# An S4 layer and a gated MLP on one core: one long convolution through DRAM replaced by two causal blocks of 1024 tokens with dense DFTs on chip, and a decay table in polar form

## The chip, the cores and the metric

The kernel runs on one core of one Trainium2 chip. The metric is the device time of one execution in microseconds (us); a figure for a kernel is the median of its runs. The span in a profile is the time from the first to the last instruction.

The engines are PE (matrix products), DVE (elementwise work), ACT (table functions and copies), POOL and SP (issues most DMAs). "PEld" is the load of PE's weights, which overlaps PE.

## The reference

One sequence of L = 2048 tokens, D = 640 channels, N = 128 states per channel, MLP width F = 1728, bf16 in and out:

```python
def _A_ref(u, ...):                       # S4 layer
    dt = exp(log_dt)[:, None]
    P = exp((dt * A)[:, :, None] * l)     # A complex, D x N; l = 0..2047
    K = einsum("dn,dnl,dn->dl", Cc, P, dt * Bc).real     # one kernel of 2048 taps per channel
    y = irfft(rfft(pad(u)) * rfft(pad(K)))[:L]           # causal convolution along the tokens
    return y + u * Dskip

h  = x + _A_ref(layernorm(x))
h2 = h + (sigmoid(n @ w_gate) * (n @ w_up)) @ w_down     # n = layernorm(h)
```

## The kernel before

The channels are handled in four chunks of 160. Per chunk, the taps come from two tables of powers, A (32 exponents) and B (21 exponents), multiplied on PE. Table A is built on DVE by doubling: from 5 seeds, each step multiplies the powers known so far by one of them.

```python
def chain_a(c):                                   # table A by doubling, all on DVE
    for d0, n, s0, b in A_STEPS:                  # n = 1, 3, 7, 15
        ...
        for ri in range(2):
            V(t[:, ri], A[:, ri, :, s0:s1, :], bc(A[:, 1, :, b:b + 1, :], [P, G, n, 4]), ALU.mult)
        for ri in range(2):
            V(A[:, ri, :, d0:d1, :], A[:, ri, :, s0:s1, :], bc(A[:, 0, :, b:b + 1, :], [P, G, n, 4]), ALU.mult)
        V(A[:, 0, :, d0:d1, :], A[:, 0, :, d0:d1, :], t[:, 1], ALU.subtract)
        V(A[:, 1, :, d0:d1, :], A[:, 1, :, d0:d1, :], t[:, 0], ALU.add)
```

The convolution is one transform of length 4096, in two stages, and its data go through DRAM between the stages, forward and back:

```python
def u_s1():                                       # forward, stage 1
    for r in range(16):
        ...                                       # matmuls with F1, copies on ACT
        sy.dma_start(d1u[:, r]..., stg[:])        # to DRAM
def u_s2(half):                                   # forward, stage 2
    for gr in range(8):
        sy.dma_start(a2g[:], dv[...])             # back from DRAM
        sy.dma_start(W2[...], cd["W2"][...])      # twiddles, loaded each time
        ...                                       # matmuls of 64 columns of weights
        nc.scalar.copy(xu[:, QPOS[q], :, :], ps[:, :, 0:UH])
def kspec(c, kv, xu, mks, dve_add):
    def front(i0, nq, tag):                       # kernel spectrum and products
        sy.dma_start(W3[...], cd["W3"][...])
        ...                                       # 5 x 2 matmuls of 160 columns per group
        nc.scalar.copy(xk, ps)
        nc.vector.tensor_tensor(t1[:], xq, xk[:], ALU.mult)
        nc.vector.tensor_tensor(t2[:], xq, xk[:, :, ::-1, :], ALU.mult)
    def back(qp, prods, W3, extra):               # inverse, stage 1
        ...
        sy.dma_start(d2[c][4 * qp:4 * qp + 4]..., stg[:])     # to DRAM
```

The second inverse stage (`is2_row`) and the skip `u * Dskip` (rows on DVE) stand in the MLP, token group by token group. The MLP has four turns of 512 tokens: gate and up matmuls, sigmoid on ACT, their product `ml_hm` on DVE, the down matmuls.

Of the kernel before, what the change touches and what calls it, by code (L numbers as in the profile page):

```python
# [9 lines left out]
F32, BF16, I32 = DT.float32, DT.bfloat16, DT.int32  # L10
# [5 lines left out]
D = 640  # L16
MAGIC = 12582912.0
SIN_SCALE = float(np.nextafter(np.float32(2.0 * PI), np.float32(0.0))) * 2.0 ** -32
CH = ((0, 160), (160, 160), (320, 160), (480, 160))
NC = len(CH)  # L20
WM = max(w for _, w in CH)
UH = 320
LAG = 2


B_VAL = [0, 4, 2, 6, 1, 5, 3, 7, 256, 260, 258, 262, 512, 516, 768, 772, 1024, 1280, 1536, 1792, 2048]
A_EXP = [16, 8, 4, 2, 1, 3, 6, 5, 7] + [8 + x for x in (4, 2, 1, 3, 6, 5, 7)] + [16 + x for x in (8, 4, 2, 1, 3, 6, 5, 7)] + [24 + x for x in (4, 2, 1, 3, 6, 5, 7)] + [0]
A_SHIFT = (7, 6, 5, 4, 3)
M_SHIFT = (0, 1, 2, 8, 9, 10)

A_STEPS = ((5, 1, 4, 3), (6, 3, 3, 2), (9, 7, 2, 1), (16, 15, 1, 0))
B_STEPS = ((1, 2, (0, 1, 1), 2), (2, 4, (0, 2, 1), 1), (4, 8, (0, 4, 1), 0), (8, 12, (0, 4, 1), 3), (12, 16, None, 4),
           (16, 18, (0, 16, 8), 5), (18, 21, (12, 17, 2), 5))
QORD = [16] + list(range(16))
QPOS = {q: i for i, q in enumerate(QORD)}


def host_consts():
    tau = 2 * np.pi
    k32 = np.arange(32)  # L40

    F1 = np.zeros((2, 32, 4, 4, 32))
    ang = tau * np.outer(k32, k32) / 64
    re, im = np.cos(ang), -np.sin(ang)
    im[:, 0] = np.cos(tau * k32 * 32 / 64)
    for q in range(4):
        F1[0, :, q, q, :] = re
        F1[1, :, q, q, :] = im
    F1 = F1.reshape(2, 128, 128).transpose(1, 0, 2)

    l2a = (16 * np.arange(4)[None, :] + np.arange(16)[:, None]).reshape(-1)
    k1 = np.arange(34)[:, None]
    k2 = np.arange(64)[None, :]
    phi = tau * l2a[:, None, None] * (k1 + 64 * k2)[None] / 4096
    c, sn = np.cos(phi), np.sin(phi)
    W2 = np.zeros((2, 64, 2, 34, 64))
    W2[0, :, 0], W2[1, :, 0], W2[0, :, 1], W2[1, :, 1] = c, sn, -sn, c
    W2[1, :, :, 0] = 0
    W2[1, :, 0, 32], W2[1, :, 1, 32] = c[:, 32], -sn[:, 32]
    W2[0, :, :, 32] = 0  # L60
    W2[:, :, :, 33] = 0

    kp, kk2 = np.arange(128) >> 6, np.arange(128) & 63
    q17 = np.arange(17)[None, :, None]
    l2b = np.arange(64)[None, None, :]
    psi = tau * l2b * (2 * q17 + kp[:, None, None] + 64 * kk2[:, None, None]) / 4096
    c, sn = np.cos(psi), np.sin(psi)
    W3a = np.concatenate([c, sn], axis=2)
    W3b = np.concatenate([-sn, c], axis=2)
    W3a[0:64, 0, 64:], W3b[0:64, 0, 64:] = 0, 0  # L70
    W3a[0:64, 16], W3b[0:64, 16] = np.concatenate([0 * c[0:64, 16], c[0:64, 16]], 1), np.concatenate([0 * c[0:64, 16], -sn[0:64, 16]], 1)
    W3 = np.stack([W3a, -W3a, W3b], axis=1)

    ang = tau * np.outer(k32, k32) / 64
    wre = 2 * np.cos(ang)
    wre[0] = 1
    wim = -2 * np.sin(ang)
    wim[0] = np.cos(tau * 32 * k32 / 64)
    W4 = np.zeros((32, 2, 2, 2, 32, 4))
    for qi in range(2):  # L80
        for qp in range(2):
            W4[:, 0, qi, qp, :, 2 * qi + qp] = wre / 4096
            W4[:, 1, qi, qp, :, 2 * qi + qp] = wim / 4096
    W4 = W4.reshape(128, 2, 128)
    sel = np.zeros((128, 4, 128))
    for i in range(4):
        sel[0:i + 1, i, 127] = 1.0
    lr = np.arange(2048).astype(np.float32).astype(ml_dtypes.bfloat16).astype(np.int64)
    f = np.arange(34)[:, None] + 64 * np.arange(64)[None, :]
    E = np.exp(-2j * np.pi * (np.arange(2048)[:, None] * f.reshape(1, -1) % 4096) / 4096)  # L90
    S = np.zeros((2049, f.size), np.complex128)
    np.add.at(S, lr, E)
    S = S.reshape(2049, 34, 64)
    S[:, 33] = 0
    M = np.zeros((17, 4, 32, 2, 5, 128))
    a = np.arange(32)
    for m in range(4):
        for j in range(5):
            blk = S[B_VAL[4 * j + m] + 8 * np.array(A_EXP)].reshape(32, 17, 128).transpose(1, 0, 2)
            M[:, m, :, 0, j] = blk.real  # L100
            M[:, m, :, 1, j] = blk.imag

    pick = np.zeros((128, 4, 32))
    for c in range(4):
        pick[4 * a + c, c, a] = 1.0
    last = np.zeros((128, 4, 4))
    for c in range(4):
        last[124 + c, c, :] = 1.0
    return {"pick": pick.reshape(128, -1), "last": last.reshape(128, -1), "ident": np.eye(128), "F1": F1.reshape(128, -1), "W2": W2.reshape(128, 2, 17, 2, 64)[:, :, QORD].transpose(0, 2, 1, 3, 4).reshape(128, -1), "W3": W3[:, :, QORD].transpose(0, 2, 1, 3).reshape(128, -1),
            "W4": W4.reshape(128, -1), "sel": sel.reshape(128, -1), "M": M.reshape(17, 128, 1280)[QORD].transpose(1, 0, 2).reshape(128, -1)}  # L110
# [27 lines left out]
def full_kernel(tc, ins, out):  # L138
    nc = tc.nc
    sc = Scope(tc)  # L140
    sy = nc.sync
    x2d = ins["A_u"].rearrange("b l d -> (b l) d")
    o2d = out.rearrange("b l d -> (b l) d")
    xv, ov = x2d.rearrange("(p r) d -> p r d", r=16), o2d.rearrange("(p r) d -> p r d", r=16)
# [3 lines left out]
    d1u = dram.tile([2, 16, P, D], BF16, name="d1u")  # L148
    d2 = [dram.tile([32, P, w], BF16, name=f"d2_{i}") for i, (_, w) in enumerate(CH)]

    cp = sc.pool("consts", bufs=1, side="right")
    tabp = sc.pool("tables", bufs=1, side="right")
    xp = sc.pool("xp", bufs=1)
    xup = sc.pool("xup", bufs=2)
    stp = sc.pool("stg", bufs=3)
    ktp = sc.pool("kts", bufs=2)
    kw2 = sc.pool("kw2", bufs=2)
    w3p = sc.pool("w3", bufs=3)
# [3 lines left out]
    def cload(pool, n, shape):  # L162
        t = pool.tile(shape, BF16, name="c_" + n)
        flat = t[:] if len(shape) == 2 else t[:].rearrange("p a b -> p (a b)") if len(shape) == 3 else t[:].rearrange("p a b c -> p (a b c)")
        sy.dma_start(flat, cd[n])
        return t

    u = xp.tile([P, 16, D], BF16, name="u", tag="X0")
    ef = xp.tile([P, 7, D], F32, name="ef", tag="X1")
# [3 lines left out]
    def load_u(rg):  # L173
        sy.dma_start(u[:, 4 * rg:4 * rg + 4, :], xv[:, 4 * rg:4 * rg + 4, :])
# [8 lines left out]
    for rg in range(1, 4):  # L183
        load_u(rg)
    F1 = cload(cp, "F1", [P, 2, P])
    W4 = cload(cp, "W4", [P, 2, P])
    sel = cload(cp, "sel", [P, 4, P])
    pick = cload(cp, "pick", [P, 4, 32])
    last = cload(cp, "last", [P, 4, 4])
    uh = cp.tile([4, D], BF16, name="uhead")  # L190
    kr = cp.tile([4, D], F32, name="klast_f")

    nc.scalar.activation(dl[:, 1], dl[:, 0], AF.Exp)
    diag = stp.tile([P, 5, 128], BF16, name="diag", tag="st")
    nc.vector.tensor_tensor(diag[:], bc(ident[:].rearrange("p (o n) -> p o n", o=1), [P, 5, 128]), bc(dl[:, 1].rearrange("p (c o) -> p c o", o=1), [P, 5, 128]), ALU.mult)
# [4 lines left out]
    def scaled(terms):  # L200
        pt = ps2.tile([P, 2, 512], F32, name="pt", tag="p2")
        pf = pt[:].rearrange("p a b -> p (a b)")
        for c in range(5):
            for i, (src, dg) in enumerate(terms):
                nc.tensor.matmul(pf[:, 128 * c:128 * c + 128], lhsT=src[:, c, :], rhs=dg[:, c, :], start=(i == 0), stop=(i == len(terms) - 1))  # L205
        return pf[:, 0:D]
# [4 lines left out]
    ph = scaled([(raw[:, 0, 1], diag)])  # L211
    TURN = 2.0 ** 32 / (2.0 * PI)
    nc.vector.tensor_scalar(rnd, ph, TURN, MAGIC * 2.0 ** 32, ALU.mult, ALU.add)
    nc.vector.tensor_scalar(rnd, rnd, MAGIC * 2.0 ** 32, None, ALU.subtract)
    phi = tabp.tile([P, D], I32, name="phi")
    nc.vector.scalar_tensor_tensor(phi[:], ph, TURN, rnd, ALU.mult, ALU.subtract)

    T = {}

    def exps(c):  # L220
        o, w = CH[c]
        T["E"] = E = tabp.tile([P, 11, WM], BF16, name="tabE")
        for i, k in enumerate(M_SHIFT + A_SHIFT):
            nc.scalar.activation(E[:, i, 0:w], lre[:, o:o + w], AF.Exp, scale=float(2 ** k))
# [3 lines left out]
    def cb_product():  # L228
        c1, c2 = ef[:, 3:5], ef[:, 5:7]
        B, C = raw[:, 1], raw[:, 2]  # L230
        f = lambda t: t.rearrange("p a b c -> p a (b c)")
        g = lambda t: t.rearrange("p b c -> p (b c)")
        nc.vector.tensor_tensor(c1, f(B), f(C), ALU.mult)
        nc.vector.tensor_tensor(c2[:, 0], g(B[:, 0]), g(C[:, 1]), ALU.mult)
        nc.vector.tensor_tensor(c2[:, 1], g(B[:, 1]), g(C[:, 0]), ALU.mult)
        blk = lambda t: t.rearrange("p (b c) -> p b c", c=128)
        for ri, (t, dg) in enumerate(((c1, (0, 1)), (c2, (0, 0)))):
            nc.scalar.copy(CB[:, ri, :], scaled([(blk(t[:, i]), diagf[:, dg[i]]) for i in range(2)]))

    NDV = 8  # L240
    mv = cp.tile([P, 16, 2], F32, name="mv")
    rstd = cp.tile([P, 16], F32, name="rstd")
    nmr = cp.tile([P, 16], F32, name="nmr")
# [196 lines left out]
    def kspec(c, kv, xu, mks, dve_add):  # L440
# [52 lines left out]
        for i, *pw in queue:  # L493
            back(i, *pw, None if i else extra)
            yield
# [347 lines left out]
```

## Time and profile before

| | before |
|---|---|
| time, median of 3 runs | 430.27 us (429.46 to 431.82) |
| span in the profile | 425.9 us |
| front: up to the first gate matmul | 229.1 us |
| MLP: from there to the end | 196.8 us |
| moved by DMA | 52.03 MB |

I cut the span where the first gate matmul starts (the table of stretches is cut 0.2 us later, at 229.3), since different engines limit the two sides. The table of stretches of the kernel before gives, per stretch, the busy time of each engine with its count of instructions, then the granted PE clock (as a share of full speed), the DMA share and GB/s:

```profile
core 0: us, PE busy (x) PEld busy (x) DVE busy (x) ACT busy (x) POOL busy (x), PEclk, DMA share, GB/s
0.00:229.30 229.30, 157.75 (x1926) 120.03 (x1928) 188.30 (x445) 167.00 (x309) 8.94 (x31) 0.84 0.58 169
229.30:425.90 196.60, 191.18 (x1089) 101.59 (x1100) 94.59 (x188) 47.20 (x75) 4.71 (x5) 0.99 0.23 68
```

In the MLP PE is busy 191 of 197 us at nearly full clock, which makes it the limit there. Over the whole front no engine is full: DVE has 188 of 229 us, ACT 167. DVE's other 41 us lie mostly at the two ends: from 40 to 180 us it is busy 132 of 140 us. The DMAs show in the chain of waits of the kernel before (shares of the span by engine), and in what PE's matmuls wait for, here three groups (line, engine, operation, out and in, count; busy us and mean ns; idle before it and what ended that):

```profile
PE 55%; DVE 23%; DMA 11%; ACT 5%; issue 2%; POOL 1%; SPq 1%; DVEq 0%; ACTq 0%; POOLq 0%
...
L451 PE MATMUL ps_xk<-kv,mk 128*128 128x160 bf16 x680 | 52.4, 236 | 2.2 <-ACT kv L416 1.2
...
L479 PE MATMUL ps_g<-t,W3g 64*128 64x160 bf16 x462 | 25.3, 244 | 12.1 <-DVE t L458 5.2
...
L382 PE MATMUL ps_s<-a2g,W2g 128*64 128x320 bf16 x136 | 17.4, 388 | 10.9 <-DMA W2g<-s4c_W 7.5
```

DMA has 11% of the chain, 47 us: apart from the first load of `u` (5.1 us), these are the trips through DRAM and the twiddles. The largest groups of table A, from the list of groups with each shape apart:

```profile
L331 DVE TENSOR_TENSOR tabA<-tabA 128x2400 bf16<-128x2400 bf16 x8 | 11.2, 1402 | 0.0
L329 DVE TENSOR_TENSOR tS<-tabA 128x2400 bf16<-128x2400 bf16 x8 | 10.9, 1402 | 0.0
```

Summed over its shapes, the doubling of table A is 65 us of DVE, a third of DVE's work in the front.

### The profile page before, as it was taken

How to read it: one execution, taken by the hardware profiler on the slowest of the kernel's cores; microseconds unless marked ns; L12 is line 12 of the kernel's file. 1: busy time of each engine (PE TensorE's matmuls, PEld its weight loads, DVE VectorE, ACT ScalarE, POOL GpSimd, SP SyncE). 2: the span in 40 equal slices, each digit the busy share in tenths (PEclk: the TensorE clock that was granted, in tenths of full speed). 3: DMA queues.
4: the chain of work that ended last, by engine and by line, in shares of the span. 5: the costliest groups of instructions: out<-in, count | busy, mean ns of one | idle time of the engine just before them, and what ended most of it. 6: DMA issues, size and time to landing. Idle time of an engine off the chain costs nothing.

```text
span 425.9 us, 7734 instructions
## 1 busy us (share of the span) xinstructions
PE 348.9 (82%) x3013; PEld 221.6 (52%) x3028; DVE 282.9 (66%) x633; ACT 214.2 (50%) x383; POOL 13.6 (3%) x36
## 2 busy tenths in 40 slices
PE   1615656697968979789647999999999999999996
PEld 0602235286728858678424444654466445654463
DVE  4978999979998999937723589426932386223331
ACT  6799987995798955544525525322210212012210
POOL 0011000000000000000002001000100000000000
PEclk9976658599788989989986999999999999999999
DMA  8564649865472551649628998010001000010001
GB/s 190 223 237 147 214 146 333 267 186 124 108 219 81 127 130 45 160 106 256 190 51 261 306 299 222 0 63 1 1 2 53 11 0 2 2 62 0 2 15 48
DMA packets 71108, 52.03 MB, mean 122 GB/s; under 512 B 42016, under 2 KB 68896, under 8 KB 71072
## 3 DMA queue, kind: packets, MB, share of 16 engines
q1 hardware_dynamic: 71072, 51.53, 41.3%
q8 instruction: 24, 0.39, 0.4%
q14 instruction: 12, 0.10, 0.1%
HBM read 38.41 MB, written 13.11 MB: 121 GB/s over the span
## 4 chain that ended last, share of the span: by engine, by line
PE 55%; DVE 23%; DMA 11%; ACT 5%; issue 2%; POOL 1%; SPq 1%; DVEq 0%; ACTq 0%; POOLq 0%
PE ml_po L767 13%; PE ml_pg L731 13%; PE ml_pu L731 12%; DMA W2g<-s4c_W 4%; PE ps_xk L451 3%; DVE tS L329 3%; PE pk L401 3%; DVE tabA L331 2%; DVE t L458 2%; DVE t L459 2%; PE ps_y L505 2%; PE pt L205 2%; PE ml_pt L713 2%; DVE tS L351 2%; DMA d1u<-s_stg 2%
## 5 line engine op out<-in xcount | busy, mean ns | idle before, releaser
L739 ACT ACTIVATE ml_sg<-ml_pg 128x512 bf16<-128x512 f32 x52 | 31.0, 597 | 119.6 <-PE ml_pg L731 119.6
L740 DVE TENSOR_TENSOR ml_hm<-ml_pu,ml_sg 128x512 bf16<-128x512 f32 x52 | 35.5, 682 | 49.2 <-PE ml_pu L731 49.1
L731 PE MATMUL ml_pg<-lnT,Wg 128*128 128x512 bf16 x251 | 65.2, 383 | 0.5
L731 PE MATMUL ml_pu<-lnT,Wu 128*128 128x512 bf16 x256 | 64.8, 380 | 0.4 <-issue 0.2
L767 PE MATMUL ml_po<-Wd,ml_hm 128*128 128x320 bf16 x416 | 60.1, 299 | 0.0
L451 PE MATMUL ps_xk<-kv,mk 128*128 128x160 bf16 x680 | 52.4, 236 | 2.2 <-ACT kv L416 1.2
L451 PEld LDWEIGHTS <-mk 128*128 128x128 bf16 x680 | 48.0, 99 | 5.6 <-issue 2.7
L767 PEld LDWEIGHTS <-ml_hm 128*128 128x128 bf16 x416 | 39.8, 98 | 17.5 <-issue 2.1
L731 PEld LDWEIGHTS <-Wu 128*128 128x128 bf16 x260 | 25.5, 98 | 30.4 <-issue 0.3
L731 PEld LDWEIGHTS <-Wg 128*128 128x128 bf16 x260 | 25.3, 99 | 29.1 <-issue 1.1
L780 DVE TENSOR_TENSOR ml_out<-ml_po,h 128x640 bf16<-128x640 f32 x16 | 13.2, 825 | 38.6 <-PE ml_po L767 21.1
L479 PE MATMUL ps_g<-t,W3g 64*128 64x160 bf16 x462 | 25.3, 244 | 12.1 <-DVE t L458 5.2
L362 PE MATMUL ps_s<-u,c_F 128*128 128x320 bf16 x64 | 18.0, 402 | 19.7 <-ACT s_stg L363 14.3
L453 ACT CAST xk<-ps_xk 128x640 bf16<-128x640 f32 (+1 forms) x36 | 23.7, 664 | 17.0 <-PE ps_xk L451 14.5
L479 PEld LDWEIGHTS <-W3g 64*128 64x128 bf16 x462 | 17.8, 99 | 18.1 <-issue 11.3
L482 ACT CAST g_stg<-ps_g 128x640 bf16<-128x640 f32 x32 | 22.3, 697 | 8.6 <-DMA d<-g_stg 5.2
L382 PE MATMUL ps_s<-a2g,W2g 128*64 128x320 bf16 x136 | 17.4, 388 | 10.9 <-DMA W2g<-s4c_W 7.5
L401 PE MATMUL pk<-tabB,tabA 128*128 128x84 bf16 x320 | 21.1, 235 | 4.1 <-DVE tabA L332 1.7
L362 PEld LDWEIGHTS <-c_F 128*128 128x128 bf16 x64 | 7.4, 118 | 29.3 <-issue 21.0
L401 PEld LDWEIGHTS <-tabA 128*128 128x128 bf16 x320 | 18.4, 120 | 8.2 <-issue 7.7
L384 ACT CAST xu<-ps_s 128x640 bf16<-128x640 f32 x34 | 21.3, 700 | 2.6 <-PE ps_s L382 2.5
L458 DVE TENSOR_TENSOR t<-xu,xk 128x640 bf16<-128x640 bf16 (+1 forms) x36 | 16.9, 470 | 6.8 <-ACT xk L453 6.6
(119 smaller groups left out, 493.7 us busy)
## 6 DMA issues: line engine op xcount, KB each, us to landing
W3g<-s4c_W SPq DMA_DIRECT2D x32, 192.0 KB, 2.8
d1u<-s_stg SPq DMA_DIRECT2D x16, 320.0 KB, 2.3
a2g<-d1u SPq DMA_DIRECT2D x16, 320.0 KB, 4.3
d<-g_stg SPq DMA_DIRECT2D x32, 160.0 KB, 2.5
g<-d SPq DMA_DIRECT2D x16, 320.0 KB, 6.0
mk<-s4c_M SPq DMA_DIRECT2D x5, 960.0 KB, 7.2
u<-in_A_u_dram SPq DMA_DIRECT2D x4, 640.0 KB, 5.3
h<-in_A_u_dram SPq DMA_DIRECT2D x4, 640.0 KB, 5.9
```

The lines of the kernel that those rows point to most:

```text
L362: nc.tensor.matmul(ps[:, ri, 0:UH], lhsT=F1[:, ri, :], rhs=u[:, r, o:o + UH], start=True, stop=True)
L384: nc.scalar.copy(xu[:, QPOS[q], :, :], ps[:, :, 0:UH])
L401: nc.tensor.matmul(pk[:, i, :], lhsT=A[:, ri, g].rearrange("p e c -> p (e c)"), rhs=B[:, ri, :, 4 * g:4 * g + 4], start=(ri == 0), stop=(r ...
L451: nc.tensor.matmul(ps[:, qi, ri * w:ri * w + w], lhsT=mks[i0 + qi][:, ri, j, :], rhs=kv[:, j, :], start=(j == 0), stop=(j == 4))
L453: nc.scalar.copy(xk[:].rearrange("p q r w -> p q (r w)"), ps[:, 0:nq, 0:2 * w])
L458: nc.vector.tensor_tensor(t1[:], xq, xk[:], ALU.mult)
L479: nc.tensor.matmul(ps[:, kpar, qi * w:qi * w + w], lhsT=Wt[sl, ti, wi, :], rhs=t[sl, ti, ro, :], start=(i == 0), stop=(i == cnt[kpar] - 1) ...
L482: nc.scalar.copy(stg[:].rearrange("p (q k) w -> p k q w", k=2), ps[:, :, 0:2 * w].rearrange("p k (q w) -> p k q w", q=2))
L731: nc.tensor.matmul(ps[:], lhsT=W[:, dc, f0:f0 + 128], rhs=rhs, start=(dc == 0), stop=(dc == 4))
L739: nc.scalar.activation(sg[:], pg[:], AF.Sigmoid)
L740: nc.vector.tensor_tensor(hm[:, ft, :], pu[:], sg[:], ALU.mult)
L767: nc.tensor.matmul(po[k][:, c, 0:320], lhsT=hm[:, ft, 128 * lr:128 * lr + 128], rhs=Wd[:, ft, 320 * c:320 * c + 320], start=(start and ft ...
```

## The change

Its intent: replace the trips through DRAM by dense DFTs of 1024 tokens on chip, two causal blocks of them; build table A with much less DVE work, as magnitude times cosine and sine; and move part of the convolution under the MLP, where DVE and ACT have room.

- A block's tokens and their reversal are added and subtracted (`fold`), and multiplied with a dense real matrix G (`forward`). Block 0's spectrum stays in SBUF; block 1's goes to DRAM for later use.
- Table A's entry is exp(8k Re) times cos and sin of a phase; exponents 16 to 31 reuse the same cosines and sines (`table_a`). For that the phases are counted from the middle of the table, and the phase of the middle is put into the product C times B.
- `Dskip` is added to tap 0 by one small matmul.
- Only the first block's products and inverse (`kspec`, `inv0`) stand before the MLP. Those of the second block (`products1`, `inverse1`) are given a priority 1200 places later and run in turns 0 and 1 of the MLP.

The core of the diff (cuts marked):

```diff
+    def trig_a(c):
+        ...
+        for k0, n in ((0, 6), (6, 5), (11, 5)):
+            for k in range(n):
+                nc.vector.tensor_scalar(ph[:, k], phi[:, o:o + W], 4.0 * (31 - 2 * (k0 + k)) * 2.0 ** -32, MAGIC16, ALU.mult, ALU.add)
+            p16 = ...                                # low 16 bits: the phase as int16
+            act_fn(f(sn), p16, AF.Sin, scale=SIN_SCALE16)
+            cos_of(f(cs), p16, SIN_SCALE16)          # ACT: Abs in place, then Sin
+    def table_a(c, parts=1):
+            ...
+            V(hi[:, 0], E[:, :, ::-1, :], bc(T["E16"]..., [P, n, 16, 4]), ALU.mult)
+            V(hi[:, 1], hi[:, 0], sn, ALU.mult)
+            nc.vector.tensor_scalar(hi[:, 1], hi[:, 1], -1.0, None, ALU.mult)
+            V(hi[:, 0], hi[:, 0], cs, ALU.mult)
+            V(lo[:, 1], E, sn, ALU.mult)
+            V(lo[:, 0], E, cs, ALU.mult)
-    def chain_a(c):
-        ...
-    def u_s1():
-        ...
-    def u_s2(half):
-        ...
+    def fold(b):
+        ...
+        V(pm[:, 0], u[:, b, 0], u[:, b, 1][:, ::-1], ALU.add)
+        V(pm[:, 1], u[:, b, 0], u[:, b, 1][:, ::-1], ALU.subtract)
+    def forward(b, pm, Z):
+        ...                                          # 8 matmuls of 320 columns per PSUM tile
+                    nc.scalar.copy(zs[...] if b else Z[...], ps[:, :, 0:UH])
+                if b:
+                    sy.dma_start(dz1[ft, :, hf], zs[:])
...
+    for c in range(NC - 1):
+        if c:
+            kvs.append(kmm(c))
+            inv0(c - 1, Vt)
+        table_a(c + 1, 2 if c == NC - 2 else 1)
+        if c + 2 < NC:
+            trig_b(c + 2)
+            open_b(c + 2)
+            bases_b(c + 2)
+            chain_b(c + 2)
+            if c == 0:
+                exps_a(1)
+            trig_a(c + 2)
+        corner(c)
+        Vt = kspec(c, kvs[c][0], KM, Z0, vp, yp)
...
+    tc.cur_priority += LATER                         # LATER = 1200
+    block1()                                         # products1, 8 times
+    tc.cur_priority -= LATER
...
+            if rc == 1 and ft < 8:
+                inverse1(ft // 4, ft % 4, pso_p)
```

## The prediction

> **What bounds it now.** The stretch table splits the 425.9 us span at 229.3 us, where the first gate matmul starts. Front (0 to 229.3): DVE busy 188.3 us, ACT 167.0, PE 157.8 at a granted clock of 0.84. From 40 to 180 us DVE is busy 132 of 140 us: it is the limit, with DMA waits between (11% of the chain of waits: a2g, W2g, W3g, g). MLP (196.6 us): PE busy 191.2 us, clock 0.99: PE is the limit; DVE has 94.6 us of work.
>
> **DVE, front.** Issue-to-issue costs from the timeline: bf16 tensor_tensor 0.40 us for 640 elements, 0.74 for 1280, 1.32 for 2400. Table A's doubling chain costs 65 us busy, plus 4.6 for its seeds (groups summed). It becomes, per chunk, five 2560-element tensor_tensor (1.4 us each) and one negation, some 31 us in all. tensor_tensor stays in 2x mode (Trainium skill, "VectorE: DVE Perf Modes", the perf-mode tier table; the trace agrees: 1280 elements per 0.67 us above a fixed part). Added: 64 phase reductions (0.15 us each, for 20 shifts, +7), block sums and differences (+6), turning CB (+3). Spectral products go from 39 to 31 us: only block 1's are in the front. In the program's order this sums to 159 us of DVE issue time before the MLP, against about 183.
>
> **PE, front.** kspec goes from 680+462 matmuls of 160 columns (71 to 87 ns apart) to 320, plus about 270 in the inverse; forward DFTs from 200 to 288 of 320 columns (0.138 us at full clock): 30 to 40 us less. The chirp through DRAM goes, with most loads on the chain. ACT: 34 fewer forward and 24 fewer output evictions (0.65 us each), but more sines and exponentials: about -15 us.
>
> **DVE stays the front's limit**: tables and products of chunks 1 to 3 run back to back. With the idle at start and end (about 20 us) and 5% between, the first gate matmul comes at about 190 us.
>
> **MLP.** PE gains 136 matmuls of 320 columns (+18.8 us) and loses 54 (-7). A bare turn is 44.2 us (the last, in the chain); with transposes 45.4. Sum: 45.4+64+45.4+48 = 203 us. The new load is DVE: eight product steps, each 12 tensor_tensor of 640 and two of 1280 elements, 6.3 us, 51 us in all, in turns 0 and 1 beside hm (0.60 each). By the program's order DVE ends the last step about 82 us after the MLP's start; PE wants it at about 76. I expect 5 us of PE stall: MLP 208 us.
>
> **Total.** 190+208 = 398 us span, plus 4 us between span and measured time: 402 us, range 385 to 421. Faster by over 2%: 0.90; within 2%: 0.07; slower: 0.03.
>
> **Right if**: first gate matmul at 180 to 205 us; DVE busy over 85% from 40 to 150 us; kspec group 320 matmuls; MLP stretch 203 to 215 us, with PE waiting for DVE only in turn 1; DMA under 5% of the chain.
>
> **Wrong if**: loads of KM (2.6 MB) collide with the writes of block 2's spectrum and stall the second forward DFT (I allow 4 us); the reloads of spectrum and kernel queue behind 7.7 MB of MLP weights and products start late; table accesses in runs of 4 lose 2x mode (+30 us); the indirect reversed load is slow; PE gets half clock in gaps (before: 0.54 to 0.67 from 25 to 80 us), as "TensorE: Matmul & The Clock Gate", Part 1, says of idle windows.

## The result, and the profile after

| | before | after |
|---|---|---|
| time, median | 430.29 us (4 runs) | 403.10 us (402.66 to 404.71, 4 runs) |
| ratio | | 0.9373, 95% interval 0.9338 to 0.9408 |
| span in the profile | 425.9 us | 401.3 us |
| front | 229.1 us | 193.0 us |
| MLP | 196.8 us | 208.3 us |
| moved by DMA | 52.03 MB | 38.91 MB |

A ratio is the mean time of one kernel's fast runs over that of the other's in the same rounds, so it is not quite the ratio of the medians that I quote.

The front is 36.1 us shorter and the MLP 11.5 us longer. The two spans thus differ by 24.6 us, not by the 27.2 of the medians, because the profile before was taken, by its span, in one of that kernel's faster runs. The table of stretches of the changed kernel, with three stretches more:

```profile
core 0: us, PE busy (x) PEld busy (x) DVE busy (x) ACT busy (x) POOL busy (x), PEclk, DMA share, GB/s
0.00:193.00 193.00, 134.95 (x1512) 110.66 (x1513) 163.91 (x417) 152.81 (x266) 11.37 (x16) 0.88 0.41 141
193.00:401.30 208.30, 203.02 (x1185) 109.91 (x1182) 122.54 (x246) 37.57 (x63) 2.01 (x2) 0.99 0.17 57
...
40.00:120.00 80.00, 60.81 (x560) 45.84 (x558) 73.77 (x189) 74.42 (x120) 3.69 (x2) 0.83 0.33 126
100.00:120.00 20.00, 11.59 (x97) 10.13 (x96) 16.33 (x50) 19.49 (x29) 0.00 (x0) 0.51 0.21 83
239.90:307.60 67.70, 66.30 (x406) 37.24 (x404) 52.71 (x117) 9.52 (x16) 2.01 (x2) 1.00 0.14 40
```

Of the front's shortening (36.3 us between the cuts of the two tables), 24.4 us are less busy time of DVE (188.3 to 163.9) and 11.9 less idle time of DVE (41.0 to 29.1). But the third row says something that the whole front does not: from 40 to 120 us DVE and ACT are equally full, 74 of 80 us each. Between 100 and 120 us it is ACT that is full, and PE works little over half the time, at half clock. The last row is turn 1 of the MLP with the second block's inverse in it: PE is busy 66.3 of 67.7 us.

The chain of waits of the changed kernel, and the groups that answer to those shown before:

```profile
PE 52%; DVE 34%; ACT 8%; DMA 2%; issue 2%; POOL 1%; SPq 0%; DVEq 0%; POOLq 0%; ACTq 0%
...
L466 PE MATMUL ps_xk<-kv,KM 128*128 128x160 bf16 x320 | 27.8, 248 | 12.7 <-ACT xk L467 10.6
...
L499 PE MATMUL ps_y<-V,c_IV 128*128 128x160 bf16 x256 | 21.8, 248 | 1.9 <-DVE V L451 1.9
...
L610 PE MATMUL ps_y<-Z,c_IV 128*128 128x320 bf16 x128 | 19.6, 299 | 1.4 <-DVE Z L451 1.4
```

DMA fell from 11% of the chain to 2%. The kernel spectrum has 320 matmuls in place of 680. Its PE time waits 10.6 us for ACT, where before it waited for almost nothing. The same chain read in order of time (start, us, what), in one stretch of the front:

```profile
35.81 1.40 DVE pm L378
37.32 6.60 ACT ln_junk L361 x16
43.93 0.98 ACT a_cs L224
44.91 0.76 ACT a_sn L224
46.02 0.99 ACT a_ph L246
47.59 10.25 PE ps_z L390 x56
57.87 0.69 ACT Z L393
58.56 0.91 ACT tabMB L224
59.50 0.66 DVE tabMB L264
60.16 1.43 DVE u L375 x4
```

Here the chain changes hands every few microseconds: DVE, then ACT (layer norm statistics and sines), then PE, then ACT, then DVE. This is a part with much ACT in it. Summed over the front's 193 us, the pieces of the chain are 93 us of DVE, 48 of PE and 30 of ACT: DVE has the most, but less than half. Table A with each shape apart:

```profile
L288 DVE TENSOR_TENSOR tabA<-tabEA,tabE 128x2560 bf16<-128x2560 bf16 x3 | 4.5, 1489 | 4.1 <-PE pk L412 4.1
...
L290 DVE TENSOR_SCALAR tabA<-tabA 128x2560 bf16<-128x2560 bf16 x3 | 2.4, 812 | 0.0
...
L246 ACT ACTIVATE a_ph<-a_ph 128x960 int16<-128x960 int16 x4 | 5.2, 1295 | 0.0
```

Per chunk, five products of 2560 elements, 1.48 us each (1.40 from issue to issue), and one negation do the work of the doubling. (The last chunk's are made in two halves.) For all four chunks these are 33 us, and the 64 phase reductions (`a_ph`) add 12, against 65 us for the doubling. The layout in runs of 4 did not cost tensor_tensor its double rate. The Trainium skill's "VectorE: DVE Perf Modes", in the perf-mode tier table, allows tensor_tensor that rate at most on bf16 and tensor_scalar twice that; the trace agrees, 1.49 us against 0.81 for the negation.

### The profile page after: what moved, and what is told of

It is laid out like the page before. It is cut to its first block, busy times and chain, and to the rows that moved or that the text cites. A ratio compares the mean times of both kernels' runs of the same rounds, so it can differ in the third digit from the quotient of the medians.

```text
span 401.3 us, 6771 instructions
## 1 busy us (share of the span) xinstructions
PE 338.0 (84%) x2694; PEld 220.6 (55%) x2694; DVE 286.4 (71%) x663; ACT 190.4 (47%) x328; POOL 13.4 (3%) x18
## 2 busy tenths in 40 slices
DMA packets 27393, 38.91 MB, mean 97 GB/s; under 512 B 8161, under 2 KB 19938, under 8 KB 26978
## 3 DMA queue, kind: packets, MB, share of 16 engines
q0 software_dynamic: 288, 1.31, 0.9%
## 4 chain that ended last, share of the span: by engine, by line
PE 52%; DVE 34%; ACT 8%; DMA 2%; issue 2%; POOL 1%; SPq 0%; DVEq 0%; POOLq 0%; ACTq 0%
PE ml_pg L713 12%; PE ml_pu L713 12%; PE ml_po L751 11%; PE ps_y L499 4%; DVE u L598 3%; PE ps_xk L466 3%; PE ps_z L390 3%; DVE tS L342 2%; DVE tabB L343 2%; PE ps_y L610 2%; DMA u<-in_A_u_dram 2%; ACT ln_junk L361 2%; DVE a_ph L273 2%; DVE ln_st L351 2%; ACT xk L467 2%
## 5 line engine op out<-in xcount | busy, mean ns | idle before, releaser
L390 PE MATMUL ps_z<-pm,G 128*128 128x320 bf16 x256 | 44.2, 319 | 19.2 <-DVE pm L377 12.0
L390 PEld LDWEIGHTS <-G 128*128 128x128 bf16 x256 | 26.1, 103 | 32.3 <-issue 20.5
L466 PE MATMUL ps_xk<-kv,KM 128*128 128x160 bf16 x320 | 27.8, 248 | 12.7 <-ACT xk L467 10.6
L763 DVE TENSOR_TENSOR ml_out<-ml_po,h 128x640 bf16<-128x640 f32 x16 | 13.2, 822 | 31.2 <-PE ml_po L751 16.9
L466 PEld LDWEIGHTS <-KM 128*128 128x128 bf16 x320 | 25.5, 104 | 14.6 <-issue 14.0
L499 PE MATMUL ps_y<-V,c_IV 128*128 128x160 bf16 x256 | 21.8, 248 | 1.9 <-DVE V L451 1.9
L467 ACT CAST xk<-ps_xk 128x640 bf16<-128x640 f32 x32 | 20.8, 698 | 5.0 <-DVE t L476 2.1
L499 PEld LDWEIGHTS <-c_IV 128*128 128x128 bf16 x256 | 20.0, 105 | 2.6 <-issue 1.9
L610 PE MATMUL ps_y<-Z,c_IV 128*128 128x320 bf16 x128 | 19.6, 299 | 1.4 <-DVE Z L451 1.4
L610 PEld LDWEIGHTS <-c_IV 128*128 128x128 bf16 x128 | 12.1, 98 | 8.2 <-issue 1.9
L413 ACT CAST kts<-pk 128x420 bf16<-128x420 f32 x32 | 15.3, 518 | 1.7 <-PE pk L412 1.6
L342 DVE TENSOR_TENSOR tS<-tabB,tabMB 128x640 bf16<-128x640 bf16 (+3 forms) x24 | 14.3, 595 | 0.2
```

Of the source, the lines that this page charges most:

```text
L342: V(t, s, bc(M[:, 1:2, mi:mi + 1, :], [P, 2, n, W]), ALU.mult)
L390: MM(ps[:, ri, 0:UH], lhsT=G[:, ft, hf, ri, r, :], rhs=pm[:, ri, r, o:o + UH], start=(r == 0), stop=(r == 3 and not b))
L413: nc.scalar.copy(kts[:, g0:g0 + GS, :], pk[:])
L466: MM(ps[:, hf, ri * W:ri * W + W], lhsT=KM[:, ft, hf, ri, j, :], rhs=kv[:, j, :], start=(j == js[0]), stop=(j == js[-1]))
L467: nc.scalar.copy(xk[:, ft - f0, kind].rearrange("p h r w -> p h (r w)"), ps[:, :, 0:2 * W])
L499: MM(ps[:, e, tt * W:tt * W + W], lhsT=IV[:, 2 * tp + tt, e, ft, ri, :], rhs=Vt[:, ft, e, ri, :], start=False, stop=(tt == 1 and ft == 3 a ...
```

## The experiments

Twelve kernels ran, each on one chip together with the kernel before. To compare with the changed kernel I use the ratios to before; a difference of 0.01 is 4.3 us. With three rounds the interval of a ratio is some ±0.004. The difference of two kernels carries both intervals, some ±2.4 us, so smaller gains are not settled by the times alone. The comparison with the reference says little about the finer parts of the convolution.

| kernel | median, us | ratio to before | first gate matmul, us |
|---|---|---|---|
| changed kernel | 403.10 | 0.9373 | 193.0 |
| a_chain | 415.16 | 0.9640 | 206.5 |
| b_polar | 457.71 | 1.0644 | 259.5 |
| later0 | 447.09 | 1.0391 | 193.2 |
| no_prod1 | 402.25 | 0.9344 | 194.3 |
| dve_less | 399.73 | 0.9280 | 187.4 |
| act_less | 401.07 | 0.9299 | 191.4 |
| pe_less | 402.48 | 0.9350 | 193.0 |
| late_a | 402.65 | 0.9351 | 192.4 |
| both_less | 390.15 | 0.9066 | 181.1 |
| pool_ph2 | 417.28 | 0.9713 | 206.8 |
| tail | 399.41 | 0.9278 | 188.5 |
| tail_late | 397.71 | 0.9248 | 186.4 |

### One part of the change alone: a_chain and b_polar

a_chain is the changed kernel with the old doubling table; it is right.

```diff
-    def trig_a(c): ...      # 16 phases, 6 sines and 3 absolute values of up to 960 elements
-    def table_a(c, parts=1): ...
+    def trig_a(c): ...      # 5 shifts, one sine and one cosine of 800 elements
+    def table_a(c, parts=1): ...   # the seeds and the old A_STEPS
```

> The changed kernel with table A built by before's doubling chain again (correct result). Issue costs summed in its own program order: VectorE 189.4 us ahead of the first gate-times-up product, against 168.2 in the changed kernel and 185.0 in the kernel before; ScalarE about 25 us lighter than the changed kernel, TensorE the same. Theory (VectorE issue time limits the front): first gate matmul 15 to 24 us later than 193 us, time 418 to 427 us. Rival 1 (ScalarE limits it, or the gain came from the DFT and the loads that went): 400 to 408 us.

It took 415.16 us (0.964), between the two expectations: the polar table is worth 12 us in the new kernel, not the 19 by which DVE's busy time in the front differs (183.1 against 163.9). Everything else, the two-block DFT with its move under the MLP, is worth 15 us (430.3 to 415.2). The table of stretches of a_chain:

```profile
40.00:180.00 140.00, 104.52 (x1178) 84.55 (x1182) 137.12 (x295) 76.11 (x127) 2.93 (x7) 0.83 0.25 91
```

With the old table DVE really is the limit: 137 of 140 us. ACT has 76. The polar table takes work off DVE and gives ACT 33 us (190.4 busy in the whole program against 157.2), and ends with both at about nine tenths from 40 to 150 us (101.4 and 98.2 of 110). a_chain also shows the DFT's part in the chain of waits: of the front's chain, DMA has 45 us in the kernel before and 8.5 in a_chain. But PE's part falls too (53 to 32 us) and ACT's (22 to 4.5), while DVE's grows (92 to 149), so what of the 15 us is owed to the DMAs was not taken apart.

b_polar is the kernel before with the polar table; it is right.

```diff
-        bases_a(c, ga); ...; chain_a(c)
+        table_a(c, ga)              # polar, 16 exponentials per chunk on ACT
-    for i, k in enumerate(M_SHIFT + A_SHIFT):
+    for k in range(1, 16): nc.scalar.activation(E[:, :, k, :], lv, AF.Exp, scale=8.0 * k)
```

> The kernel before with the polar table A alone (correct result; phases in batches of 4 and exponentials per chunk for want of memory). VectorE issue sum to the first gate-times-up product 163.4 us against 185.0 in the kernel before; everything else of before stays, with its loads through DRAM. Theory (VectorE limits the front): 408 to 416 us, a good half of the whole gain. Rival 2 (the loads and the TensorE work of the chirp transform limit the front of before as much, so that freed VectorE time turns into waits): 420 us or more.

It took 457.71 us: 27 us slower than the kernel before. Neither expectation foresaw this: the rival's range (420 or more) contains it, but its reason, the loads and PE, is not what the trace shows. The stretches of b_polar show why:

```profile
40.00:180.00 140.00, 89.83 (x1042) 65.46 (x1042) 86.06 (x208) 135.76 (x265) 3.23 (x4) 0.73 0.51 149
```

ACT is busy 136 of 140 us and DVE 86: the limit went over to ACT. One reservation: memory was short in the old kernel, so b_polar makes table A's exponentials chunk by chunk (64 of 160 elements, where the changed kernel has 32 of 320), changes ACT's function table 17 times (the kernel before 9 times, the changed kernel 5, 1.28 us each), and has one phase buffer where that has two. A better version would lose less; how much is open. The old kernel already had ACT busy 111 of these 140 us, and the new DFT needs fewer copies out of PSUM (a_chain: 76). That this is what makes room for the sines is likely, but a better b_polar was not run. As built, the two parts of the change are not a sum: in this order they are worth 15 and 12 us, in the other −27 and +55.

### The MLP side: later0 and no_prod1

later0 sets the priority offset of the second block's products to 0; it is right.

```diff
-LATER = 1200
+LATER = 0
```

> The changed kernel with the priority offset of block 2's products set to 0 (correct result). In program order all eight product steps, 51 us of VectorE, then stand between the third and the fourth gate-times-up product of turn 0. Theory (TensorE can run only two tiles ahead of VectorE): TensorE stalls about 40 us in turn 0, turn 1 loses its 1.4 us wait, time 435 to 450 us. Rival (the offset does not matter because VectorE has 85 us to spare in the MLP): 400 to 408 us.

447.09 us (1.039): the one constant is worth 44 us. The waits of later0 hold the reason in one line (waiting engine and line, releaser; us in total, times, longest):

```profile
PE ml_pu L713 <- DVE ml_hm L722: 42.6, 1, 42.6
```

All eight product steps stand between the third and the fourth `ml_hm` of turn 0, as expected, and PE stands once for 42.6 us.

no_prod1 leaves out these products (wrong).

```diff
-        for half in range(2):
-            for ft in range(4):
-                products1(half, ft)
+        pass
```

> The changed kernel without the eight product steps of block 2 in the MLP and without their reloads (wrong result on purpose). VectorE loses 51 us of work in the MLP stretch, TensorE nothing. Theory (the products hide behind TensorE, apart from the 1.4 us wait of its trace): MLP stretch 205 to 208 us, time 400 to 403 us. Rival (my recorded 5 us stall in turn 1, or contention spread over turns 0 and 1): 396 to 399 us.

402.25 us (0.9344). 51 us of DVE's issue time, taken away (its busy time in the MLP falls from 122.5 to 75.8 us), bring about one microsecond: with the offset they are hidden under PE. In the profile the MLP is 1.9 us shorter and the front 1.2 longer; the latter was not explained.

### Which engine limits the new front: dve_less, act_less, pe_less, both_less

All four are wrong. They leave out about 13 us of one engine's issue time in the front (pe_less 12 by its expectation), or of two engines. In the traces DVE's busy time in the front falls by 13.3 us in dve_less and ACT's by 11.6 in act_less, but PE's only by 4.2 in pe_less (135.0 to 130.8): pe_less is the weaker test.

```diff
# dve_less, in chain_b
+            if n not in (2, 4):
                 V(dst[:, 0], dst[:, 0], t[:, 1], ALU.subtract)
                 V(dst[:, 1], dst[:, 1], t[:, 0], ALU.add)
# act_less, in trig_a: the sine without the Abs before it
-            cos_of(f(cs), p16, SIN_SCALE16)
+            act_fn(f(cs), p16, AF.Sin, scale=-SIN_SCALE16, bias=hpi[:, 0:1])
# pe_less, in kmm
-                    for ri in range(2):
+                    for ri in range(1):
# both_less: dve_less and act_less together
```

> The changed kernel without the subtraction and addition of table B's steps with n = 2 and n = 4 (wrong result on purpose): 13.4 us less of DVE issue time in front of the MLP, by the issue-to-issue costs read from its trace. Theory A (DVE alone is the front's limit): 10 to 14 us faster than the changed kernel's 403.1, so 389 to 393. Theory B (DVE and ACT share the limit, each waits for the other in turn, DVE being busy 102 of 110 us and ACT 98 of 110 between 40 and 150 us): 5 to 9 us faster, 394 to 398. Theory C (ACT alone): 400 or more.

> The changed kernel without the absolute value ahead of the cosines of table A (wrong result on purpose): 12 ACT instructions of 1.1 to 1.3 us fewer, some 13 us of ACT issue time, all of it in front of the MLP. Theory A (DVE alone): 0 to 3 us faster than 403.1, so 400 to 403. Theory B (shared limit): 4 to 8 us faster, 395 to 399. Theory C (ACT alone): 10 to 13 us faster, 390 to 393.

> The changed kernel with only the real half of the table product (wrong result on purpose): 160 fewer matmuls of 84 columns, 0.073 us apart, 11.7 us less PE work in front of the MLP. Theories A, B and C all say that PE is not the front's limit: 0 to 2 us faster than 403.1, so 401 to 403. If PE were on the chain there (the chain of waits of the whole program gives PE 52%, most of it in the MLP), 5 us or more would go: 398 or less.

> The two omissions together: table B's subtractions and additions in two steps (DVE, 13.4 us) and table A's absolute values (ACT, 13 us). Alone they brought 3.4 and 2.0 us of the 13 each. Theory B (DVE and ACT hold the front in turn: where one's work is taken away, the other is full, 18 to 20 of 20 us in the stretch tables of both kernels): together they bring clearly more than the sum of 5.4, 9 to 16 us, so 387 to 394. Rival D (neither engine's amount of work matters much; the front is a chain of latencies and of fixed pieces at its start and end): additive or less, 397 to 400.

By the medians dve_less brought 3.4 us, act_less 2.0, pe_less 0.6 (by the ratios 4.0, 3.2 and 1.0). So theory A fails: 13.4 us of DVE work is worth a quarter of its length. C fails too. Theory B's figures were also too high for each run alone. both_less decides between B and D: 13.0 us, where D had said 5.4 or less. By the ratios the two together bring 13.2 us against 7.2 for the sum of the single ones; the intervals of the four ratios leave 6.0 ± 3.7 us for the difference. The start of the MLP says the same: 5.6 and 1.6 us earlier alone, 11.9 together. The table of stretches from 40 to 120 us of dve_less, of act_less and of both_less:

```profile
40.00:120.00 80.00, 62.79 (x606) 47.66 (x604) 63.66 (x160) 74.51 (x122) 3.17 (x2) 0.85 0.34 126
```

```profile
40.00:120.00 80.00, 58.93 (x564) 44.71 (x565) 73.11 (x183) 66.42 (x111) 3.70 (x2) 0.86 0.33 125
```

```profile
40.00:120.00 80.00, 63.79 (x677) 48.83 (x675) 69.90 (x167) 70.04 (x123) 3.87 (x2) 0.91 0.34 126
```

In dve_less DVE falls from 74 to 64 us of this stretch and ACT stays at 74.5; in act_less it is the other way round. Where one engine is relieved, the other keeps the pace. The Trainium skill's "Perfetto Trace Analysis", under "Identifying the Most-Contended Engine", advises to take the engine with the highest occupancy first. In this front two engines stand within 1 us of each other from 40 to 120 us, and work taken off either one alone shortens the time by less than a third of its length.

pe_less also bears on a worry of the prediction. PE gets half clock in the front (0.51 from 100 to 120 us of the changed kernel), as the Trainium skill's "TensorE: Matmul & The Clock Gate", Part 1, says of a PE that has been idle; the trace agrees, for PE stood 6.5 us, from 97.6 to 104.1, waiting for ACT. By this reading the low clock is a consequence of a wait. With half of the table product's matmuls gone the first gate matmul came at the same time, 193.0 us, so at least this much of PE's work is not what the front waits for. What the low clock costs is not shown, since no run changed the clock alone.

### Another order of ACT's work: late_a

Right. The exponentials and sines for later chunks come after the kernel spectrum of the present one.

```diff
             chain_b(c + 2)
-            if c == 0:
-                exps_a(1)
-            trig_a(c + 2)
         corner(c)
         Vt = kspec(c, kvs[c][0], KM, Z0, vp, yp)
+        if c + 2 < NC:
+            if c == 0:
+                exps_a(1)
+            trig_a(c + 2)
```

> The changed kernel with one reordering, correct: the exponentials for the second half of table A and the sines of table A for two chunks ahead come after the kernel spectrum of the present chunk in the program, not before it. In the changed kernel these hold up the spectrum's evictions on ACT from 95 to 115 us, while PE waits (10.6 us put down to that wait, clock 0.51) and DVE idles 3.7 of 20 us between 100 and 120 us. Theory A (DVE alone): the DVE idle there is filled, 3 us faster at most, 400 to 403. Theory B (shared limit, ACT's order decides): 3 to 8 us faster, 395 to 400. Rival: ACT's work is only put off and then delays table A of the next chunk, same or slower, 403 to 410.

402.65 us (0.9351), half a microsecond to one: not settled by itself. ACT's work is as full as before (74.73 of 80 us from 40 to 120 us); an order cannot make it less.

### Work for the idle engine: pool_ph2

The 64 phase reductions go to POOL, which also makes the cosine's phases a quarter turn further, so that ACT needs no absolute value. It is meant to be right.

```diff
         for k0, n in ((0, 6), (6, 5), (11, 5)):
-            ph = tabp.tile([P, 6, W], F32, name="a_ph", tag="ph", bufs=2)
-            for k in range(n):
-                nc.vector.tensor_scalar(ph[:, k], ..., MAGIC16, ALU.mult, ALU.add)
-            ...
-            act_fn(f(sn), p16, AF.Sin, scale=SIN_SCALE16)
-            cos_of(f(cs), p16, SIN_SCALE16)
+            for dst, q in ((sn, 0.0), (cs, 0.25)):
+                ph = tabp.tile([P, 6, W], F32, name="a_ph", tag="ph", bufs=2)
+                for k in range(n):
+                    nc.gpsimd.tensor_scalar(ph[:, k], ..., MAGIC16 + q, ALU.mult, ALU.add)
+                ...
+                act_fn(dst[...], p16, AF.Sin, scale=SIN_SCALE16)
```

> The changed kernel with the 64 phase reductions of table A on POOL (idle in the front but for 11 us) and with the cosine's phases made there too, a quarter turn further, so that ACT needs no absolute value; meant to be right. It takes 64 x 0.15 us = 9.4 us off DVE and 13 us off ACT and gives POOL 128 instructions of 128x160, whose time no trace here shows. If POOL makes one in 0.4 us or less (12.8 us per chunk) and is not in DVE's way: 4 to 12 us faster, 391 to 399. If POOL is slower, or DVE's tensor_tensor and POOL hold each other up[...]: same or slower, 402 to 420.

417.28 us (0.9713): 14 us slower than the changed kernel, although it takes as much off ACT as act_less does, and 9 us of issue time off DVE. The groups of pool_ph2 (its L343 is L344 of the changed kernel):

```profile
L274 POOL TENSOR_SCALAR a_ph<-phi 128x160 f32<-128x160 int32 x128 | 66.4, 519 | 59.8 <-ACT tabMB L224 22.4 <-ACT a_sn L224 14.4 <-ACT a_cs L224 7.8
...
L343 DVE TENSOR_TENSOR tabB<-tabB,tS 128x640 bf16<-128x640 bf16 x12 | 6.3, 522 | 0.1
```

The same group in the changed kernel:

```profile
L344 DVE TENSOR_TENSOR tabB<-tabB,tS 128x640 bf16<-128x640 bf16 x12 | 5.8, 481 | 0.1
```

Two things went wrong. First, POOL and ACT pass two phase buffers to and fro: POOL waits for ACT 44.6 us in all, the three releasers that the line names, and ACT waits for POOL's phases 21.4 us (13.3 for the sines and 8.1 for the cosines). Second, POOL and DVE hold each other up. A reduction takes 0.37 us (median), but from 133.7 us on, beside DVE's tensor_tensor, 26 of them take 18.95 us, 0.73 each (the longest of all 128 takes 3.27). In the same stretch DVE's products of 640 elements take 0.60 us (median) in place of 0.48. So what was taken off DVE came back: it has 64 instructions fewer in the front and is busy 163.9 us there, as in the changed kernel. The Trainium skill's "SBUF — State Buffer", under "SBUF: two separate sides", says that a DVE instruction with two SBUF inputs and a POOL instruction that reads SBUF exclude one another; the trace agrees. The shares of the two causes were not taken apart.

### Another order at the seam: tail and tail_late

Between the last inverse matmul (185.7 us) and the first gate matmul (193.0) the changed kernel runs a chain of small steps. From its timeline (start, us, engine, line):

```profile
184.71 1.02 DVE L578 BATCH_NORM_STATS2 ln_st<-ps_y 128x6 f32<-128x160 f32 x4 [4.90 <-PE ps_y L499]
185.65 0.61 DVE L679 BATCH_NORM_AGGREGATE ln_mv<-ln_st 128x2 f32<-128x24 f32 x4
...
186.61 1.01 POOL L368 TENSOR_TENSOR ln_rstd<-ln_rstd,mhalf 128x4 f32<-128x4 f32 x1 [96.71 <-DVE ln_rstd L367]
...
187.91 1.73 ACT L686 ACTIVATE ln<-h,ln_nmr,ln_rstd 128x640 bf16<-128x640 bf16 x2 [0.81 <-DVE ln_nmr L369]
...
189.02 1.07 PE L698 MATMUL ml_pt<-c_ident,ln 128*128 128x128 bf16 x8 [3.24 <-DVE ln L688]
```

The first turn needs only half of the block's tokens. tail makes these first, and lets PE do the other half during the chain; it is meant to be right and removes no work. tail_late adds late_a.

```diff
-    inv0(NC - 2, Vt)
+    inv0(NC - 2, Vt, tps=(0,))
     ...
-    inv0(NC - 1, Vl, fs=((0, 1), (2, 3)), done=done)
+    inv0(NC - 1, Vl, tps=(0,), fs=((0, 1), (2, 3)), done=done)
+    inv0(NC - 2, Vt, tps=(1,))
+    inv0(NC - 1, Vl, tps=(1,))
# in the MLP
-            if rc == 0 and i % 2:
+            if rc == 0 and i == 3:          # ACT scales one row, DVE three
-            pt = psg_p.tile([P, 4, 128], BF16, name="ml_pt", tag="ml_pg")
+            pool, tag = (psu_p, "ml_pu") if rc == 0 and dc % 2 else (psg_p, "ml_pg")
+            pt = pool.tile([P, 4, 128], BF16, name="ml_pt", tag=tag)
```

> The changed kernel with another order at the seam, meant to be right: the inverse transforms of chunks 2 and 3 are made first for the tokens of the MLP's first turn and then for the others, so that PE's second half (5.6 us of matmuls) runs beside the layer norm's chain of small steps, during which PE stands idle 3.24 us in the changed kernel; ACT scales one row and not two; the first transposes use four PSUM buffers and not two. No engine's work is changed. If the seam is a chain of latencies, as the single omissions suggest (13 us less on one engine brought 2 to 3.4): the first gate matmul 3 to 5 us earlier than 193.0, time 398 to 400.5. Rival (the seam's order is hidden by what limits the whole front): 402 to 404.

> The same order at the seam together with the late sines and exponentials of late_a, which alone brought about half a microsecond. Meant to be right. If the two add: 0 to 1 us faster than the run with the seam alone, 397.5 to 400. If the late sines only shift a wait: same as the seam alone or up to 2 us slower.

tail took 399.41 us (0.9278) and tail_late 397.71 (0.9248, interval 0.9207 to 0.9288; five rounds each). Both times lie in the ranges expected. tail_late has the lowest median of the right versions: 32.6 us faster than the kernel before, 5.4 faster than the changed one. Its 1.7 us over tail are more than the 0 to 1 expected, but the intervals of the two overlap, so they are not settled. From the timeline of tail:

```profile
184.50 2.39 PE L499 MATMUL ps_y<-V,c_IV 128*128 128x160 bf16 x32
...
184.87 1.01 POOL L368 TENSOR_TENSOR ln_rstd<-ln_rstd,mhalf 128x4 f32<-128x4 f32 x1 [93.75 <-DVE ln_rstd L367]
...
186.73 1.85 PE L701 MATMUL ml_pt<-c_ident,ln 128*128 128x128 bf16 x20
```

PE runs into the transposes without idling. The edit has three parts, the order, ACT's rows and the four PSUM buffers, and no run separates them. The gate matmuls stand 5.3 us earlier in tail (the second group at 190.94 us against 196.20), but the span is only 2.7 us shorter. Most of the rest is given back in turns 0 and 1, in waits for DVE. One line of the same timeline, at the end of turn 0:

```profile
220.15 0.38 PE L701 MATMUL ml_pt<-c_ident,ln 128*128 128x128 bf16 x4 [1.53 <-DVE lnT L702]
```

The changed kernel has no such wait there. DVE, which has these copies among the second block's products, makes them late. There are two such waits, 2.1 us in all, where the changed kernel has none. PE's wait for the products themselves is no longer than before (1.42 us against 1.40). A shorter front does not by itself bring this out: in both_less the front is 11.9 us shorter and the MLP takes 208.1 us, as in the changed kernel (208.3), against 210.1 in tail.

## Why the prediction was right

The time came within 1.1 us of the figure. That it came so near is partly luck: the front was 3.0 us longer than predicted, the MLP 0.3 longer, and the step from span to time 2.2 shorter. Its terms, one by one:

- **The front's end, 190 us: 193.0.** Right within the range given.
- **"DVE stays the front's limit": only half right, and the step that failed.** DVE was busy 92% from 40 to 150 us (predicted over 85%), so the check that I had set was met. But dve_less and both_less show that DVE is the limit only together with ACT. ACT's sum was foreseen (15 us less predicted, 14 measured). What I did not ask was which of the two would be fuller between 40 and 120 us, after DVE had lost 24 us. That the front still came out near its figure is not luck, for the terms of the sum hold: DVE was busy 163.9 us (159 of issue time predicted), idle 18 us before 40 and after 180 us (about 20 predicted for start and end), and idle 11 between (11 left in the sum). Wrong was only what follows from "the limit": that DVE's work alone sets the front's length.
- **DVE's saving, 24 us of issue time: about right.** Its busy time in the front fell by 24.4. The two are not the same measure: the issue times that I summed again for a_chain, up to the first product `ml_hm`, fall by 16.8 (185.0 to 168.2).
- **PE's saving in the front, 30 to 40 us: too large.** Its busy time fell by 22.8. It seems not to have mattered: in pe_less 4.2 us less left the start of the MLP where it was.
- **DMA under 5% of the chain: right, 2%.** This came with the block DFT: a_chain has 2% too, and with DVE busy 183.1 us in the front (188.3 before) it gained 15 us.
- **MLP, 208 us: 208.3.** Two errors cancelled. The stall in turn 1 was mis-sized, 5 us predicted and 1.4 measured, and the turns without it took 4 us more than the 203 predicted: turn 0 took 46.9 us against 45.4, turn 1 66.3 against 64 (67.7 with the stall).
- **Span to time, 4 us: 1.8.** The 4 us came from a profile taken in one of the faster runs of the kernel before. The span was 401.3 us and not 398; the two errors cancel but for 1.1 us.
- **The dangers listed.** KM's loads and the reloads did not stall anything that the waits show, the tables kept their double rate, and the half clock came (0.51 from 100 to 120 us); what it cost was not measured.

The gain of 27.2 us is thus 15 for the block DFT with its move under the MLP and 12 for the polar table in its presence. No run keeps the second block in the front, so what the move alone brings is not shown; but it needs the offset: without it the whole gain is lost and 17 us more.

## What to carry to other kernels

When a change moves work from a full engine to one that is less full, add up both engines for the stretch where the work lands; here two that were both nine tenths full and fed each other paid back less than a third of what was taken from either, and half of the sum when it was taken from both. The test is cheap: leave out a known piece of each engine's work, alone and together. Where one stage hands over to the next, make first what the next stage needs first; with two smaller edits at the seam this brought about 4 us here, though the start of the next stage came 5 us earlier.

## What the Trainium skill lacked or had wrong

- "Perfetto Trace Analysis", "Identifying the Most-Contended Engine" and "Optimization Strategy": they speak of one most-contended engine per regime. A regime with two, where relieving either brings a quarter or less by the medians (3.4 us of 13.4, 2.0 of 13) and both together half (13.0 of 26.4), is not described.
- "SBUF — State Buffer" states the mutual exclusion of POOL and DVE but no cost for a small POOL instruction beside a stream of tensor_tensor: 0.37 us at the median (128x160, int32 to float32), 0.73 on average beside them, DVE's 640-element products 0.60 in place of 0.48.
- "ScalarE: Activation LUTs" has no figure for 16-bit elements with a step of two: an absolute value of 960 such int16 elements in place took 1.29 us, of 960 int32 elements 1.01 us (`b_ph`, in the list of groups of the changed kernel). A sine that only reads the same int16 elements took 1.01 us too, so the reading is not what costs; whether it is the writing was not tested.
- "ScalarE: Activation LUTs", "What ACT_TABLE_LOAD costs", adds a drain of some 1.38 us to the load's 1283 ns for every switch to another set of tables. The load takes 1283 ns here too, but the drain does not show: in the changed kernel the exponential before the load of 101.14 us ends at 101.13 and the sine after it starts at 102.44, 1.31 us later.
